# A gated mix of linear attention and a SwiGLU block on one Trainium2 core: the first two x tiles loaded as two half-height DMAs on two queues, and the large weights in more pieces

## The chip, the core and the metric

The kernel runs on one core of one Trainium2 chip. A core has a matrix engine (TensorE, PE in the profile, its weight loads PEld), a vector engine (VectorE, DVE), an activation engine (ScalarE, ACT), a general engine (GpSimd, POOL) and a small engine that here only issues transfers (SyncE, SP). ACT can issue transfers too. All of them are carried out by the core's 16 DMA engines. Every engine works through its own list of instructions in order and waits on semaphores for the others.

The metric is the time of one execution on the device in microseconds (us). Before the change, the median of three runs is 178.27 us (177.99 to 178.33).

## What is computed

x has 2048 tokens of 512 features, in bf16. The result mixes two branches token by token with a sigmoid gate:

```python
x = A_x
g = _sigmoid((x * gate_w).sum(-1, keepdims=True))
a = _A_ref(x, A_wqkv, A_wo)          # linear attention, 32 heads of 16
b = _B_ref(x, B_w1, B_w3, B_w2)      # (silu(x @ w1) * (x @ w3)) @ w2, 1376 hidden
return g * a + (1 - g) * b
```

In branch A, q and k go through phi(t) = (t + 1 where t > 0, else exp(t)) + 1e-6; the attention is linear (k and v are summed over all tokens into one small matrix for each head), divided by a denominator, and multiplied by wo.

## The kernel before

The tokens are cut into 16 tiles of 128 (t = 0 to 15), and into 4 blocks of 4 tiles. The 512 features are 4 chunks of 128 (kc = 0 to 3). The order of instructions on every engine is the order of the text: the schedule is written by hand.

*Loads.* They stand at the top, lines 121 to 158, nearly all on SP's queue (`dq`). The first is x_first (line 129): the first 256 tokens, 2 KB in each of 128 partitions, 256 KB, into the tile xN. Then come four pieces of wqk, the q and k columns of the attention weights, one for each kc (line 126), 14 transposing loads of x for tiles 2 to 15 (xT, line 123) with three plain loads of x (xN, line 141) between them, the gate column and the 96 last columns of w1 and w3 (wr, lines 143 to 147), and then the large weights: w1 and w3 in one DMA of 1280 KB each (line 150, a loop whose `cuts` are (0, KC)), wv, wo (lines 151, 152), w2 in one DMA of 1280 KB (line 154) and w2x (line 156). On ACT's queue there is one load, a small one of 12 KB: touch (line 133), the first 16 columns of the later wqk chunks, which nothing computes with. In ACT's program it stands behind a table load and a tiny activation (act_pre, line 130).

The framework that builds the kernel gives every DMA, from either queue, one of eight semaphores in turn. A DMA is issued only when the DMA that used its semaphore before it, eight places earlier, has landed. There are 72 DMAs in all.

*Start.* TensorE runs 13 warm-up matmuls on a constant (line 359), then transposes the first two tiles of x itself by multiplying xN with the identity (line 365, six of these at first, two later). VectorE and ScalarE copy the results into xT, and the first projections follow (line 183): for each kc, the k and q matmuls of tiles 0 and 1 in the order of lines 386 to 401, each kc needing its piece of wqk.

*First stage* (to about 46 us). For each tile: q and k projections (line 183), phi on ACT and DVE (lines 196 to 201), the running sum of phi(k) on POOL (line 215), and the products of x and phi(k) summed over all tokens (line 231).

*Second stage.* For each block of 512 tokens, ten steps of the SwiGLU block (lines 303 and 309 read w1 and w3), and in the first block the small matrices of the attention (line 447 reads wv, line 462 reads wo). The denominators come from zaccb, POOL's last sum, over SP's transposing DMA of line 421, then zrow (426) and zpk (427), and end in the transposed and scaled queries pqT (line 345). Then four output tiles (line 475 reads pqT, line 492 reads w2, line 278 w2x), mixed on DVE (line 498) and stored from SP (line 508).

Of the kernel before, what the change touches and what calls it, by code (L numbers as in the profile page):

```python
# [16 lines left out]
def kernel(  # L17
# [17 lines left out]
    nc = tc.nc  # L35
    P = nc.NUM_PARTITIONS
# [5 lines left out]
    KC = D // P  # L42
# [4 lines left out]
    FC = F // P  # L47
# [15 lines left out]
    w1_r = B_w1.rearrange("(kc d) f -> d kc f", d=P)  # L63
    w3_r = B_w3.rearrange("(kc d) f -> d kc f", d=P)
# [15 lines left out]
        out=bmask[:], in_=bmask[:], pattern=[[-Dh, HPC], [0, Dh]], compare_op=ALU.is_ge,  # L80
# [3 lines left out]
        out=bmask[:], in_=bmask[:], pattern=[[Dh, HPC], [0, Dh]], compare_op=ALU.is_ge,  # L84
# [22 lines left out]
    xN = consts.tile([P, NT, D], BF16, name="xN")  # L107
# [6 lines left out]
    w1 = consts.tile([P, KC, F0], BF16, name="w1")  # L114
    w3 = consts.tile([P, KC, F0], BF16, name="w3")
    w2 = consts.tile([P, FC, D], BF16, name="w2")
    xT = consts.tile([P, KC, S], BF16, name="xT")
    act_pre = consts.tile([P, 1], BF16, name="act_pre")
    dq = nc.sync
# [6 lines left out]
        dq.dma_start(out=wqk[:, kc, :], in_=wqkv_r[:, kc, 0 : 2 * D])  # L126

    x_first = x2d[0 : 2 * P, :].rearrange("(p j) d -> p j d", j=2)
    dq.dma_start(out=xN[:, 0:2, :], in_=x_first)  # L129
    nc.scalar.activation(out=act_pre[:], in_=warm[:, 0:1], func=ACT.Exp)  # L130

    touch = consts.tile([P, KC - 1, 16], BF16, name="touch")
# [9 lines left out]
    with nc.allow_non_contiguous_dma(reason="gate column"):  # L142
        dq.dma_start(
            out=wr[:, :, 2 * FR : NR], in_=gate_w.rearrange("(kc d o) -> d kc o", d=P, o=1)
        )
    dq.dma_start(out=wr[:, :, 0:FR], in_=w1_r[:, :, F0:F])
    dq.dma_start(out=wr[:, :, FR : 2 * FR], in_=w3_r[:, :, F0:F])
    for w, w_r, cuts in ((w1, w1_r, (0, KC)), (w3, w3_r, (0, KC))):
        for a, b in zip(cuts, cuts[1:]):
            dq.dma_start(out=w[:, a:b, :], in_=w_r[:, a:b, 0:F0])  # L150
    dq.dma_start(out=wv[:], in_=wqkv_r[:, :, 2 * D : 3 * D])
    dq.dma_start(out=wo[:], in_=A_wo.rearrange("(kc d) n -> d kc n", d=P))
    w2_r = B_w2[0:F0, :].rearrange("(fc f) d -> f fc d", f=P)
    dq.dma_start(out=w2[:], in_=w2_r)
    w2x_r = B_w2[F0:F, :].rearrange("(i r) d -> i (r d)", i=RP)
    dq.dma_start(
        out=w2x[:].rearrange("p r d -> p (r d)"),
        in_=w2x_r[None].to_broadcast([TPB, RP, RG * D]),
# [442 lines left out]
```

## Time and profile before

| | |
|---|---|
| median of three runs | 178.27 us (177.99 to 178.33) |
| the profiled execution's own time | 177.74 us |
| its span, first to last instruction | 176.0 us |
| SP's queue: x_first issued / issuing of w2x ends | 0.81 / 36.9 us |
| x_first from issue to landing | 2.8 us |
| wqk, four pieces, from issue to landing | 3.1, 3.7 (median), 4.1 us |
| w1, w3 from issue to landing | 7.5, 10.3 us |
| granted TensorE clock | 1.00 |

The profile is that of one execution. A row of the chain or of the timeline has the start in us from the span's beginning, the length in us, the engine (SPq and ACTq are the issuing of DMAs on SP and ACT), the line of the code, and what is written from what; "x13" means that thirteen such instructions are merged; a bracket at the end tells how long the engine had been idle and what ended that. A row of stretches has the stretch, its length, the busy time of PE, PEld, DVE, ACT and POOL with the number of instructions, the granted clock, the busy share of the DMA engines and the GB/s that they moved.

### The profile page before, as it was taken

Reading aid. Unit: us, or ns where it says so; the run is one execution under the profiler, and the core shown is the slowest. Engines: PE = TensorE matmul, PEld = TensorE weight load, DVE = VectorE, ACT = ScalarE, POOL = GpSimd, SP = SyncE. Lnnn points to the kernel's source line nnn. Section 1 sums busy time; section 2 is a strip of 40 time slices with the busy share of each in tenths; the row PEclk is TensorE's granted clock in tenths of the full one; section 3 lists DMA queues with packets and bytes.
Section 4 is the critical chain, followed back from the end, with each engine's and each line's share of the span. In section 5 each row is a group of like instructions: output and inputs, shape, how many; then the busy total and the mean of one; then the engine's idle time right before and its main releaser. Section 6 shows DMA issues by size and latency. Waiting matters only on the chain.

```text
span 176.0 us, 2668 instructions
## 1 busy us (share of the span) xinstructions
PE 171.3 (97%) x952; PEld 82.4 (47%) x969; DVE 110.5 (63%) x207; ACT 59.1 (34%) x109; POOL 63.3 (36%) x106
## 2 busy tenths in 40 slices
PE   8999999999999999999999999999999999999993
PEld 5444444444456443444444466444444444444453
DVE  0399788888764899777343477853435775344363
ACT  4364544544753533322433101224226122422000
POOL 5087656656300668586300044540000662000000
DMA  5988969997205112323200013330000233000001
GB/s 172 277 197 207 164 123 237 403 352 231 78 4 56 22 30 41 78 63 91 58 0 0 0 34 84 84 89 0 0 4 0 60 89 89 4 0 0 30 30 60
DMA packets 29360, 15.58 MB, mean 88 GB/s; under 512 B 21156, under 2 KB 27556, under 8 KB 29348
## 3 DMA queue, kind: packets, MB, share of 16 engines
q1 hardware_dynamic: 28948, 15.41, 35.1%
q8 instruction: 7, 0.11, 0.3%
q10 hardware_dynamic: 400, 0.01, 0.1%
q14 instruction: 5, 0.04, 0.1%
HBM read 8.86 MB, written 2.10 MB: 62 GB/s over the span
## 4 chain that ended last, share of the span: by engine, by line
PE 95%; DMA 2%; issue 1%; SPq 0%; DVE 0%
PE bank L303 20%; PE bank L492 20%; PE bank L309 19%; PE bank L183 16%; PE bank L231 8%; PE bank L475 8%; PE bank L245 3%; DMA wqk<-in_A_wqkv_dram 2%; PE bank L278 2%; PE bank L447 0%; SPq L129 0%; PE bank L462 0%; DVE o L498 0%; PE bank L365 0%
## 5 line engine op out<-in xcount | busy, mean ns | idle before, releaser
L315 DVE TENSOR_TENSOR hT<-bank,sg 128x512 bf16<-128x512 f32 x40 | 27.3, 682 | 31.0 <-PE bank L309 28.9
L303 PE MATMUL bank<-xT,w 128*128 128x512 bf16 x158 | 40.8, 379 | 0.2
L309 PE MATMUL bank<-xT,w 128*128 128x512 bf16 x156 | 40.5, 379 | 0.2
L314 ACT ACTIVATE sg<-bank 128x512 bf16<-128x512 f32 x40 | 23.9, 597 | 45.9 <-PE bank L303 45.9
L492 PE MATMUL bank<-w,hT 128*128 128x512 bf16 (+2 forms) x176 | 37.0, 355 | 0.5 <-issue 0.3
L337 POOL TENSOR_TENSOR pqs<-pq,rden 128x512 bf16<-128x512 bf16 x16 | 16.9, 1057 | 54.3 <-issue 46.8
L183 PE MATMUL bank<-wqk,xT 128*128 128x512 bf16 x126 | 30.2, 379 | 0.1
L215 POOL TENSOR_TENSOR zacc<-zacc,pk 128x128 f32<-128x128 f32 x56 | 23.3, 447 | 10.4 <-DVE pk L201 10.4
L492 PEld LDWEIGHTS <-hT 128*128 128x128 bf16 x180 | 16.7, 98 | 18.4 <-issue 0.8
L309 PEld LDWEIGHTS <-w 128*128 128x128 bf16 x160 | 15.7, 98 | 18.9
L303 PEld LDWEIGHTS <-w 128*128 128x128 bf16 x160 | 15.5, 98 | 18.2 <-issue 0.2
L498 DVE SCALAR_TENSOR_TENSOR o<-bank,omg_all,aga 128x512 bf16<-128x512 f32 (+2 forms) x18 | 12.4, 692 | 14.5 <-PE bank L492 11.7
L183 PEld LDWEIGHTS <-xT 128*128 128x128 bf16 x128 | 12.5, 98 | 14.9 <-issue 0.3
L322 POOL TENSOR_TENSOR pr<-pq,zb 128x512 f32<-128x512 bf16 x16 | 18.4, 1155 | 0.1
L231 PE MATMUL bank<-pk,xN 128*128 128x512 bf16 x62 | 16.3, 379 | 0.2
L475 PE MATMUL bank<-M,pqT 128*128 128x512 bf16 x61 | 15.6, 379 | 0.1
L196 ACT ACTIVATE eq<-bank 128x512 bf16<-128x512 f32 x16 | 9.4, 597 | 16.0 <-PE bank L183 14.9
L201 DVE SCALAR_TENSOR_TENSOR pk<-bank,emk 128x512 bf16<-128x512 f32 x16 | 11.1, 692 | 1.6
L196 ACT ACTIVATE ek<-bank 128x512 bf16<-128x512 f32 x16 | 9.4, 597 | 6.5 <-PE bank L183 6.5
L201 DVE SCALAR_TENSOR_TENSOR pq<-bank,emq 128x512 bf16<-128x512 f32 x16 | 11.1, 692 | 0.5
L326 DVE TENSOR_REDUCE den<-pr 128x32 f32<-128x512 f32 x16 | 10.8, 676 | 0.0
L231 PEld LDWEIGHTS <-xN 128*128 128x128 bf16 x64 | 6.3, 98 | 7.5
(54 smaller groups left out, 95.6 us busy)
## 6 DMA issues: line engine op xcount, KB each, us to landing
w<-in_B_w_dram SPq DMA_DIRECT2D x3, 1280.0 KB, 10.3
out_dram<-o SPq DMA_DIRECT2D x15, 128.0 KB, 1.9
wqk<-in_A_wqkv_dram SPq DMA_DIRECT2D x4, 256.0 KB, 3.7
xN<-in_A_x_dram SPq DMA_DIRECT2D x1, 1024.0 KB
xN<-in_A_x_dram SPq DMA_DIRECT2D x2, 256.0 KB, 2.9
xN<-in_A_x_dram SPq DMA_DIRECT2D x1, 512.0 KB, 4.2
wv<-in_A_wqkv_dram SPq DMA_DIRECT2D x1, 512.0 KB, 11.2
wo<-in_A_wo_dram SPq DMA_DIRECT2D x1, 512.0 KB, 12.2
```

The lines of the kernel that those rows point to most:

```text
L183: nc.tensor.matmul(ps[:], lhsT=xT[:, kc, t * P : (t + 1) * P], rhs=w[:, kc, :], start=(kc == 0), stop=(kc == KC - 1),)
L196: nc.scalar.activation(out=e[:], in_=ps[:], func=ACT.Exp)
L201: nc.vector.scalar_tensor_tensor(out=dst, in0=ps[:], scalar=0.0, in1=em[:], op0=ALU.max, op1=ALU.add)
L215: nc.gpsimd.tensor_tensor(out=(zaccb if t == NT - 1 else zacc)[:, cs], in0=zacc[:, cs], in1=pk[t][:, cs], op=ALU.add,)
L231: nc.tensor.matmul(bank[kc][:], lhsT=xN[:, t, kc * P : (kc + 1) * P], rhs=pk[t][:], start=(t == 0), stop=(t == NT - 1),)
L303: nc.tensor.matmul(g_ps[:], lhsT=w1[:, kc, fs], rhs=xT[:, kc, tok], start=(kc == 0), stop=(kc == KC - 1),)
L309: nc.tensor.matmul(u_ps[:], lhsT=w3[:, kc, fs], rhs=xT[:, kc, tok], start=(kc == 0), stop=(kc == KC - 1),)
L314: nc.scalar.activation(out=sg[:], in_=g_ps[:], func=ACT.Silu)
L315: nc.vector.tensor_tensor(out=hT[tb][:, fc, :], in0=u_ps[:], in1=sg[:], op=ALU.mult)
L322: nc.gpsimd.tensor_tensor(out=pr[t][:], in0=pq[:, t, :], in1=zb[:], op=ALU.mult)
L475: nc.tensor.matmul(ps[:], lhsT=pqT[:, c, ts], rhs=M2[:, c, :], start=(c == 0), stop=(c == KC - 1),)
L492: nc.tensor.matmul(ps[:, 0 : cs.stop - cs.start], lhsT=hT[tb][:, fc, tt * P : (tt + 1) * P], rhs=w2[:, fc, cs], start=(fc == 0 and not sta ...
```

## The change

The load of x_first becomes two DMAs: partitions 0 to 63 on SP's queue, and partitions 64 to 127 on ACT's, where it stands ahead of the table load and of touch. w1 and w3 come in four DMAs each, one for each kc, instead of one. w2 comes in two, of five chunks each, instead of one. The bytes and their places stay the same; the number of DMAs goes from 72 to 80. TensorE's first weight load from xN waits for two semaphores instead of one, and its first matmuls on w1, w3 and w2 wait for the pieces that they read. Nothing else in the order of any engine changes.

```diff
     x_first = x2d[0 : 2 * P, :].rearrange("(p j) d -> p j d", j=2)
-    dq.dma_start(out=xN[:, 0:2, :], in_=x_first)
+    dq.dma_start(out=xN[0 : P // 2, 0:2, :], in_=x_first[0 : P // 2])
+    nc.scalar.dma_start(out=xN[P // 2 : P, 0:2, :], in_=x_first[P // 2 : P])
     nc.scalar.activation(out=act_pre[:], in_=warm[:, 0:1], func=ACT.Exp)
...
-    for w, w_r, cuts in ((w1, w1_r, (0, KC)), (w3, w3_r, (0, KC))):
+    for w, w_r, cuts in ((w1, w1_r, range(KC + 1)), (w3, w3_r, range(KC + 1))):
         for a, b in zip(cuts, cuts[1:]):
             dq.dma_start(out=w[:, a:b, :], in_=w_r[:, a:b, 0:F0])
...
     w2_r = B_w2[0:F0, :].rearrange("(fc f) d -> f fc d", f=P)
-    dq.dma_start(out=w2[:], in_=w2_r)
+    for a, b in ((0, FC // 2), (FC // 2, FC)):
+        dq.dma_start(out=w2[:, a:b, :], in_=w2_r[:, a:b, :])
```

## The prediction

> **What bounds the kernel now.** I read the page first: busy times, then the chain that ended last.
>
> ```profile
> PE 171.3 (97%) x952; PEld 82.4 (47%) x969; DVE 110.5 (63%) x207; ACT 59.1 (34%) x109; POOL 63.3 (36%) x106
> ...
> PE 95%; DMA 2%; issue 1%; SPq 0%; DVE 0%
> ```
>
> TensorE is busy for 171.3 of 176.0 us, and the only transfer in the chain is 2%. So next I read that chain in order of time over the first 16 us, which shows where the 2% lies (start, length, what):
>
> ```profile
> 0.81 0.39 SPq L129
> 1.20 0.06 issue
> 1.26 3.11 DMA wqk<-in_A_wqkv_dram
> 4.37 0.04 issue
> 4.41 1.02 PE bank L183 x4
> 5.43 0.11 PE bank L365 x2
> 5.54 3.60 PE bank L183 x16
> ```
>
> After 4.41 us everything is TensorE work, one matmul behind the other. Eight matmuls take 1.73 us all along the chain, 0.216 each. The sixteen here should take 3.45 and take 3.60, so 0.15 us is lost in them. The timeline of the first 14 us says where, and what TensorE did before:
>
> ```profile
> 0.84 2.93 PE L359 MATMUL bank<-const-bfloat16-1.0 128*128 128x256 bf16 x13 [0.84 <-PEq L585]
> 0.86 0.43 ACTq L133 DMA_DIRECT2D touch<-in_A_wqkv_dram  x1
> ...
> 3.64 0.55 PEld L365 LDWEIGHTS <-xN 128*128 128x128 bf16 x6 [0.35 <-DMA xN<-in_A_x_dram]
> 3.65 0.72 PE L365 MATMUL bank<-ident,xN 128*128 128x128 bf16 x6
> ...
> 6.83 1.82 PEld L183 LDWEIGHTS <-xT 128*128 128x128 bf16 x9 [0.27 <-issue]
> ```
>
> Thirteen warm-up matmuls run until the x tiles land; the first weight load out of xN then starts at 3.64 after 0.35 us of waiting. The 0.15 us lie at 6.83: the fourth piece of wqk is issued at 2.67 and lands up to 4.1 us later (the longest of line 126), at 6.78. From 6.83 on the matmuls follow each other to the end. The change therefore can act on the end in two ways: by moving the start of that stream, or by making a weight so late that it opens a hole in it.
>
> **The change, part by part.** *The first x DMA in two halves.* One issue of 0.39 us on SP (line 129) becomes one of 64 rows on SP and one of 64 rows on ACT. Per issue I take 0.39 to 0.43 (lines 129 and 133); SP has as many issues in this stretch as before, so wqk starts at 1.26 as before. On ACT, by the order of its instructions, the new issue stands ahead of the table load and act_pre (0.80 to 2.30 now); these end 0.43 later, at 2.73, and touch starts about 0.45 later. ACT's first work for the path comes at 4.08, so 1.3 us of cover remain. Without that cover the cost would be the 0.43.
>
> What counts is when the later half lands, since TensorE's first load of xN now waits for both. At best both land before the warm-up ends. The thirteen take 2.93 us, one takes 0.42, so they start 0.209 apart, the last at 3.35, and the next could start at 3.56 instead of 3.65: a gain of at most 0.09. At worst the half on ACT's queue is as late as touch, today's only DMA there: issued at 0.86 and landed after 3.0 us although it is only 12 KB, while x with 256 KB needs 2.8. Issue at 0.82, 3.0 us, and 128 KB at the best rate seen here (413 GB/s, next fence), 0.32, give 4.14, which is 0.50 after the 3.64 of now. I take 0.0: the same 256 KB pass the same engines, and touch came late because x's bytes lay before it, not because the queue slept; in the stretch 2.5 to 3.1 us, in which x's last bytes pass, ACT's queue already moves 156 packets.
>
> ```profile
> 1.80:2.00 0.20, 0.20 (x3) 0.14 (x2) 0.00 (x0) 0.20 (x1) 0.14 (x1) 1.00 0.14 31
> 2.00:2.20 0.20, 0.20 (x3) 0.14 (x2) 0.00 (x0) 0.19 (x2) 0.19 (x1) 1.00 0.45 133
> 2.20:2.40 0.20, 0.20 (x3) 0.14 (x2) 0.00 (x0) 0.10 (x1) 0.15 (x1) 1.00 0.93 143
> 2.40:2.60 0.20, 0.20 (x3) 0.14 (x2) 0.00 (x0) 0.00 (x0) 0.17 (x1) 1.00 0.77 246
> 2.60:2.80 0.20, 0.20 (x3) 0.14 (x2) 0.00 (x0) 0.00 (x0) 0.12 (x2) 1.00 0.81 317
> 2.80:3.00 0.20, 0.20 (x3) 0.14 (x2) 0.00 (x0) 0.00 (x0) 0.20 (x1) 1.00 1.12 413
> ```
>
> These are stretches of 0.2 us; the last column is GB/s, the one before it the DMA engines' share. The load starts slowly and reaches its full rate only at 2.8, and 256 KB have passed by about 3.0.
>
> The Trainium skill (SBUF — State Buffer, section "Can I just issue two DMAs to hit both halves?") speaks against this part: a tile in partitions 0 to 63 reaches half of the memory's ports, and two concurrent DMAs on the two halves measured only 6% over one. No transfer of 64 partitions is in this trace, so nothing here shows it; by that rule the sum would be the first rival's, below.
>
> *wqk behind it.* The fourth piece sets the 0.15 us at 6.83. If it lands earlier the most to gain is that 0.15; if x's engines are held longer, it slips by as much. I take 0.0: the bytes ahead of it are the same.
>
> *w1 and w3 in four pieces, w2 in two.* Seven more issues on SP at 0.506 (line 150) are 3.5 us of queue. w1 lands at 26.4 + 7.5 = 33.9, w3 at 26.9 + 10.3 = 37.2, wv at 38.7, w2 at 30.3 + 13.5 = 43.8; they are first used at 45.9 (line 303), 46.8 (309), 52.7 (447) and 67.0 (492). So 3.5 us more leave at least 6 us for each. Each issue waits until the DMA eight places before it has landed (the order of SP's instructions with their waits). Before, all those were long landed; now wv, wo, both halves of w2 and w2x wait for pieces of w1 and w3. If the last of them, w2x, had to wait for all of w3 (37.2, plus its own 2.95 of issuing, line 156), SP would be free at 40.2, with 3.5 more at 43.7. What stands behind it is the transpose of zaccb:
>
> ```profile
> SPq L421 <- POOL zaccb L215: 9.1, 1, 9.1
> ```
>
> SP sits 9.1 us waiting for POOL there, until 46.1. So this costs nothing; were the cover gone, zaT, zpk and pqT would slide, and the first pqT (63.6 + 2.4 = 66.0) still has 4.9 us until line 475 reads it at 70.9. The first matmuls on w1 and w3 get a wait on each piece; waits already satisfied do not show in the stream today (the 0.216 hold at every wait on an xT). With 80 DMAs for 72, eight more, every DMA behind w2x keeps the semaphore it had.
>
> Sum: 0.0 for x (from -0.09 to +0.50), 0.0 for wqk (from -0.15 to +0.15), 0.0 for the weights: 176.0 + 0.0 in the span and 1.7 around it, 177.74 in the profiled execution's own time. That execution was 0.5 below the median of the three runs, 178.27, so in their terms 178.3.
>
> **The rivals.** *Halves at half rate: slower.* Place: the load of x. If a DMA on 64 partitions can use half of the path, the six rows above are capped at half of 413, 207 GB/s. By 2.4 us 61 KB have passed below that cap; the other 201 KB then need 0.97 us and end at 3.37 instead of 3.02: +0.35. If the slow start is not cover but comes on top (1.1 us now against 0.63 at 413, so 0.47 lost; 1.27 at 207), they end at 3.66: +0.64. wqk lies behind on the same engines and slips as far, so all of it reaches the end: 178.6 to 178.9, say 178.75. It decides from the moment x lands after 3.64, one for one, and can be measured from 0.36 later, 4.0. For it: the rows from 2.6 on do run above 207. Against: the first half of the load does not, and the two halves together use everything. The rule named above is this case.
>
> *ACT's queue starts late: slower.* The half on ACT lands at 4.14 as worked out. wqk does not slip then, so its 0.15 is absorbed: +0.35, 178.6. For it: touch's 3.0 us. Against: touch stands behind act_pre in ACT's order, the new DMA stands first.
>
> *A better start: faster.* The two queues fill the slow rows 1.8 to 2.6 together, x lands before the warm-up ends and wqk before 6.6: -0.24 in all, 178.0. More than this is only possible if the start of an ordinary run is worse than that of the profiled one, which the 0.5 between them leaves open. Against: the warm-up's 3.56 is a floor.
>
> *The pieces hold SP beyond 46.1 by more than the 4.9 us of slack.* Each microsecond beyond is one of the end; 179 or more. Against: six microseconds of margin ahead of that.
>
> **How the numbers follow.** No change worth measuring 0.44; half rate 0.28; ACT late 0.11; better start 0.15; SP held 0.02. A measurement of this kernel can tell about 0.2%, 0.36 us, from nothing. Of the likeliest, 0.38 lies within that and 0.03 on each side; of half rate 0.20 above it, of ACT late 0.07; of the better start 0.12 below; SP held above. Faster 0.15, within 0.53, slower 0.32. The likeliest alone would be 178.0 to 178.5 (-0.24 to +0.2). The range goes to 178.85 to hold the most of the two slower cases, and to 177.85 for the better start with the spread of the three runs (0.34) under it.
>
> **What would show it.** In the profile after: the first weight load out of xN at 3.6 (right), about 4.0 to 4.3 (half rate, with wqk's pieces later too), about 4.1 with wqk where it was (ACT late), or 3.55 (better start); the idle time before the fourth piece of wqk; SP's wait for zaccb still above 2 us; no idle time at the first matmuls of lines 303, 309, 447 and 492. A hole in the stream after 7 us, or a total that moves without the first 7 us moving, would make the prediction wrong.

## The result, and the profile after

| | before | after |
|---|---|---|
| median of six executions | 178.19 us (177.83 to 178.33) | 180.98 us (179.08 to 181.24) |
| the profiled execution | 177.74 us | 181.11 us |
| its span | 176.0 us | 179.3 us |

The changed kernel takes 1.0123 times as long as the one before (95% interval 1.0099 to 1.0147). It is slower, and it lies well above the range of the prediction. Its executions fall into two groups, two at 179.1 us and four from 180.93 to 181.24; the profile is one of the upper group. The ratios in this document are those on record, which are not quotients of the medians (180.98/178.19 would be 1.0157).

The page after has the same make-up as before, but the transfer in the chain that ended last has grown from 2% to 3%:

```profile
PE 173.8 (97%) x969; PEld 82.9 (46%) x969; DVE 110.3 (62%) x207; ACT 59.1 (33%) x109; POOL 63.2 (35%) x106
...
PE 95%; DMA 3%; SPq 0%; DVE 0%; issue 0%
```

VectorE, ScalarE and GpSimd are busy as long as before, within 0.2 us. TensorE is busy 2.5 us longer with the same work. Some matmul records are missing before (hence x952), which makes part of that; but 1.5 us of it are on the line of the projections (30.2 before, 31.7 now) for two records more, so TensorE was slower there. The chain of waits over the first 16 us says where (start, length, what):

```profile
1.44 4.92 DMA wqk<-in_A_wqkv_dram
...
6.40 1.87 PE bank L185 x4
...
8.48 3.87 PE bank L185 x16
...
13.00 0.86 PE bank L185 x4
```

Two things are new. The first projection (line 185, line 183 before) starts at 6.40 instead of 4.41, because wqk's first piece takes 4.92 us instead of 3.11 and is issued 0.18 later. And the first four projections then take 1.87 us, where four of the same kind take 0.86 at 13.00. The timeline of the first 14 us shows what came ahead of it (start, length, engine, line, what is written from what; the bracket is the idle time before and what ended it):

```profile
0.81 0.58 SPq L129 DMA_DIRECT2D xN<-in_A_x_dram  x1
0.81 0.55 ACTq L130 DMA_DIRECT2D xN<-in_A_x_dram  x1
...
1.44 2.23 SPq L126 DMA_DIRECT2D wqk<-in_A_wqkv_dram  x4
...
4.18 0.56 PEld L367 LDWEIGHTS <-xN 128*128 128x128 bf16 x6 [0.88 <-DMA xN<-in_A_x_dram]
...
6.40 1.87 PE L185 MATMUL bank<-wqk,xT 128*128 128x512 bf16 x4 [1.39 <-DMA wqk<-in_A_wqkv_dram]
```

Each half of x takes 0.55 to 0.58 us to issue, where the whole took 0.39. The first weight load out of xN starts at 4.18 instead of 3.64, and TensorE then waits another 1.39 us for wqk.

Nothing behind this adds to it. I take the first projection of tile 3, the twenty-first matmul of its line, as a mark: it starts at 9.63 us before and at 12.84 after, and from there to the end of the span are 166.41 us before and 166.42 after. In all seventeen profiles of this study that rest lies between 166.4 and 166.7 us. So all but 0.3 us of the difference between any two of these profiles is made before the mark or outside the span, and the experiments can be read there. Of the 3.37 us between the two profiled executions, 1.99 is the later first projection, 1.21 is the slower stretch from it to the mark (6.43 instead of 5.22 us), 0.01 is the rest, and 0.15 lies outside the span (1.85 instead of 1.70 us).

### The profile page after: what moved, and what is told of

Its sections match the earlier page's. It is cut to its first block, busy times and chain, and to the rows that moved or that the text cites. A ratio compares the mean times of both kernels' runs of the same rounds, so it can differ in the third digit from the quotient of the medians.

```text
span 179.3 us, 2693 instructions
## 1 busy us (share of the span) xinstructions
PE 173.8 (97%) x969; PEld 82.9 (46%) x969; DVE 110.3 (62%) x207; ACT 59.1 (33%) x109; POOL 63.2 (35%) x106
## 4 chain that ended last, share of the span: by engine, by line
PE 95%; DMA 3%; SPq 0%; DVE 0%; issue 0%
PE bank L494 19%; PE bank L305 19%; PE bank L311 19%; PE bank L185 16%; PE bank L477 8%; PE bank L233 8%; PE bank L247 3%; DMA wqk<-in_A_wqkv_dram 3%; PE bank L280 2%; PE bank L449 0%; SPq L129 0%; PE bank L464 0%; DVE o L500 0%; PE bank L367 0%
## 5 line engine op out<-in xcount | busy, mean ns | idle before, releaser
L305 PE MATMUL bank<-xT,w 128*128 128x512 bf16 x160 | 41.1, 379 | 0.0
L311 PE MATMUL bank<-xT,w 128*128 128x512 bf16 x160 | 41.1, 379 | 0.0
L494 PE MATMUL bank<-w,hT 128*128 128x512 bf16 (+2 forms) x180 | 37.5, 355 | 0.0
L185 PE MATMUL bank<-wqk,xT 128*128 128x512 bf16 x128 | 31.7, 391 | 1.4 <-DMA wqk<-in_A_wqkv_dram 1.4
L477 PE MATMUL bank<-M,pqT 128*128 128x512 bf16 x64 | 16.1, 379 | 0.0
```

Source lines behind the costliest of these rows:

```text
L185: nc.tensor.matmul(ps[:], lhsT=xT[:, kc, t * P : (t + 1) * P], rhs=w[:, kc, :], start=(kc == 0), stop=(kc == KC - 1),)
L305: nc.tensor.matmul(g_ps[:], lhsT=w1[:, kc, fs], rhs=xT[:, kc, tok], start=(kc == 0), stop=(kc == KC - 1),)
L311: nc.tensor.matmul(u_ps[:], lhsT=w3[:, kc, fs], rhs=xT[:, kc, tok], start=(kc == 0), stop=(kc == KC - 1),)
L477: nc.tensor.matmul(ps[:], lhsT=pqT[:, c, ts], rhs=M2[:, c, :], start=(c == 0), stop=(c == KC - 1),)
L494: nc.tensor.matmul(ps[:, 0 : cs.stop - cs.start], lhsT=hT[tb][:, fc, tt * P : (tt + 1) * P], rhs=w2[:, fc, cs], start=(fc == 0 and not sta ...
```

## The experiments

The theory at the start was that the two halves of x make it land later and wqk with it; the rivals were the pieces of w1, w3 and w2, ACT's queue, and TensorE's own rate. In each group below the kernels ran on one chip beside the kernel before (medians 178.25, 178.20, 178.13 and 178.27 us). The diffs are against the kernel before, unless said.

### Which part: e1 to e4

e1 has only x's part of the change, e2 only that of the weights:

```diff
 # e1_x_only
-    dq.dma_start(out=xN[:, 0:2, :], in_=x_first)
+    dq.dma_start(out=xN[0 : P // 2, 0:2, :], in_=x_first[0 : P // 2])
+    nc.scalar.dma_start(out=xN[P // 2 : P, 0:2, :], in_=x_first[P // 2 : P])
```

> Only the load of x is split in two halves on two queues; w1, w3 and w2 stay whole. Theory A (the whole loss comes from the split of x, in the first 9 us): 179 to 181.2, the first weight load from xN at about 4.2 and the first projection at 5 to 6.4. Rival B (the pieces of w1, w3 and w2 and their waits take a part): 178.2 to 178.6.

```diff
 # e2_w_only, against the kernel after
-    dq.dma_start(out=xN[0 : P // 2, 0:2, :], in_=x_first[0 : P // 2])
-    nc.scalar.dma_start(out=xN[P // 2 : P, 0:2, :], in_=x_first[P // 2 : P])
+    dq.dma_start(out=xN[:, 0:2, :], in_=x_first)
```

> Only w1, w3 and w2 are cut in pieces; x is one DMA of 128 partitions as before. Theory A: 178.2 within 0.3, with no idle time at the first matmuls on w1, w3 and w2. Rival B: 179 or more.

e3 puts both halves on SP's queue, e4 keeps the two queues but cuts x by columns, so that each DMA has all 128 partitions with rows of 1 KB:

```diff
 # e3_both_sp
-    dq.dma_start(out=xN[:, 0:2, :], in_=x_first)
+    dq.dma_start(out=xN[0 : P // 2, 0:2, :], in_=x_first[0 : P // 2])
+    dq.dma_start(out=xN[P // 2 : P, 0:2, :], in_=x_first[P // 2 : P])
 # e4_cols
-    dq.dma_start(out=xN[:, 0:2, :], in_=x_first)
+    dq.dma_start(out=xN[:, 0, :], in_=x_first[:, 0, :])
+    nc.scalar.dma_start(out=xN[:, 1, :], in_=x_first[:, 1, :])
```

> x in the same two halves of 64 partitions, but both on SP's queue, one after the other; weights whole. Theory C (a transfer of 64 partitions runs at half rate): x lands 0.3 to 0.7 later than the 3.60 of before, 178.6 to 179.5. Theory D (the loss comes from issuing on two queues at once, which delays the half on SP and the wqk pieces behind it): x and wqk land within 0.4 of before (one more issue of SP, 0.4, stands ahead of wqk), 178.2 to 178.7, and no late landing of the first wqk piece.

> x in two DMAs on the two queues, but each of all 128 partitions with one token row of 1 KB in each; weights whole. Theory C (64 partitions are slow): x lands as before at about 3.6, 178.2 within 0.4. Theory D (two queues at once are slow): x lands at 4.1 or later and the first wqk piece after 5, 179 or more.

| | median, us | ratio to before | first load of xN | first projection |
|---|---|---|---|---|
| e1 | 179.36 | 1.0065 [1.0032, 1.0097] | 4.02 | 5.25 |
| e2 | 178.40 | 1.0006 [0.9984, 1.0028] | 3.62 | 4.38 |
| e3 | 180.47 | 1.0107 [1.0076, 1.0138] | 4.54 | 5.18 |
| e4 | 178.60 | 1.0007 [0.9988, 1.0026] | 3.71 | 4.63 |

The cost is in x's part alone: neither the weights' pieces nor two DMAs on two queues (e4) cost anything that can be told from nothing. Two halves on one queue cost no less than on two (the intervals of e3 and e1 overlap), so ACT's queue is not what makes the change slow. Both theories for e3 had expected less, at most 179.5. The profiled execution of e3 is the fastest of its six (179.04 us, the others took 180.12 to 180.63). Its chain of waits shows five issues in a row, two of x and three of wqk:

```profile
0.81 0.58 SPq L129
...
1.45 0.57 SPq L130
...
2.07 0.58 SPq L126
...
2.70 0.42 SPq L126
...
3.17 0.43 SPq L126
...
3.64 4.34 DMA wqk<-in_A_wqkv_dram
...
8.02 2.32 PE bank L184 x10
```

Both halves are dear to issue (0.58, 0.57), and so is the first piece of wqk behind them (0.58, the next ones 0.42 and 0.43), which is a DMA of 128 rows as it was. The fourth piece is issued at 3.64 instead of 2.67 and holds TensorE until 8.02.

### touch, and the rate of TensorE: e5 to e8

e5 is e1 and e6 the kernel before, both without touch, which nothing computes with:

```diff
 # e5_x_notouch (with the edit of e1) and e6_before_notouch
-    touch = consts.tile([P, KC - 1, 16], BF16, name="touch")
-    nc.scalar.dma_start(out=touch[:], in_=wqkv_r[:, 1:KC, 0:16])
```

> x split as in the change, weights whole, and the load touch (which nothing computes with) left out. If touch, which ACT now issues at 1.45 beside SP's first wqk piece, is what makes that piece's issue 0.81 long and holds some of the DMA engines, the issue falls to about 0.4 to 0.6, wqk lands by 5, and the time falls from the 179.4 of the split alone to 178.6 to 179. If touch has no part in it: 179.2 to 179.6.

> The kernel before without touch, as the control of the run above: 178.2 within 0.3 if touch does nothing for wqk; 178.6 or more if the wqk pieces get later without it.

e5 took 178.92 us, 1.0053 [1.0019, 1.0087], and e6 178.40, 1.0011 [0.9998, 1.0024]. In e5 the first piece of wqk still takes 0.81 us to issue, as in e1. So touch is not what makes the issues dear; without it the ratio is not told apart from e1's. The time fell where it had been expected if touch mattered (178.6 to 179), but the sign that was to go with it, a shorter issue, did not come.

e7 fills the two holes of the changed kernel with warm-up matmuls, and e8 makes a hole in the kernel before and leaves its DMAs alone:

```diff
 # e7_after_fill, against the kernel after
-    warm_step(13)
+    warm_step(16)
...
+    warm_step(6)
     for kc in range(2):
 # e8_few_warm
-    warm_step(13)
+    warm_step(6)
```

> The changed kernel with TensorE kept busy on the constant while it waits: 16 warm-up matmuls instead of 13, and 6 more between the transposes and the first projection. Nothing is computed differently. Theory E (the holes at the start also keep TensorE at half rate for longer): the matmuls of line 185 are at 0.216 apart by 7 us at the latest, and the time falls from 181.0 by 0.8 to 1.5, to 179.5 to 180.2. Rival (the rate has nothing to do with the holes): 180.8 to 181.5, since fillers only add work.

> The kernel before with 6 warm-up matmuls instead of 13, so that TensorE has a hole from 2.1 to 3.6 us and all the DMAs are untouched. Theory E: x and wqk land as before, but the first projections run 0.43 apart until 7 to 9 us, and the time is 179 to 180.3. Rival: 178.2 within 0.3.

e8 took 179.52 us, 1.0076 [1.0049, 1.0103]. The chain of e8:

```profile
0.81 2.87 DMA xN<-in_A_x_dram
...
4.55 1.79 PE bank L183 x4
...
6.55 5.03 PE bank L183 x16
```

x lands at 3.68 instead of 3.60 and the first projection starts at 4.47 instead of 4.41 (timeline), yet the sixteen behind the first four take 5.03 us instead of 3.60: with seven warm-up matmuls fewer, and so a hole in TensorE's work from 2.3 to 3.7 us, its matmuls start 0.427 us apart, not 0.216, until about 9.7 us. The reverse is e7, whose chain is:

```profile
5.06 0.91 PE bank L361 x6
5.97 0.86 PE bank L185 x4
...
6.95 3.45 PE bank L185 x16
```

Without holes the first four take 0.86 and the sixteen 3.45, the full rate from the start, although the first projection starts late (5.81 in the timeline). e7 took 179.20 us (178.83 to 179.63), 1.0058 [1.0038, 1.0077]. That is less than either expectation for it (179.5 or more). It has no execution in the upper group, where the changed kernel had four of six; on another chip, though, it had two of ten (e12, below), and at that share six executions without one come about one time in four. Also, its fillers last longer than the wait that they fill, and its median is no better than that of e12 (179.10). So e7 shows the rate in one execution, not a mended kernel.

The granted clock does not show the slow stretch. These are stretches of the changed kernel (the columns are those of the stretches before the prediction; the clock is third from the end):

```profile
6.40:8.20 1.80, 1.80 (x6) 0.70 (x6) 0.00 (x0) 0.00 (x0) 0.00 (x0) 1.00 1.55 149
9.30:12.30 3.00, 3.00 (x16) 1.37 (x14) 1.19 (x3) 1.08 (x2) 0.14 (x1) 1.00 0.83 207
```

Six matmuls in 1.8 us, two of them small, and sixteen in 3.0 us, both at 1.00. The Trainium skill (TensorE: Matmul & The Clock Gate, section "Part 1: The HAM clock gate (the "warmup" mystery)") says that the array runs at half its clock until enough work has been seen in a window that runs freely, and that the number of slow matmuls therefore differs from execution to execution. The factor of two agrees with the starts here (0.427 us apart against 0.216), and so does the spread; that it is this gate no run here shows.

### How x is cut: e9 to e12

```diff
 # e9_wqk_act: x whole on SP; wqk's pieces 0 and 2 on ACT's queue, 1 and 3 on SP's
-    def load_wqk(kc):
-        dq.dma_start(out=wqk[:, kc, :], in_=wqkv_r[:, kc, 0 : 2 * D])
+    def load_wqk(kc, q=dq):
+        q.dma_start(out=wqk[:, kc, :], in_=wqkv_r[:, kc, 0 : 2 * D])
...
     dq.dma_start(out=xN[:, 0:2, :], in_=x_first)
+    load_wqk(0, nc.scalar)
...
-    for kc in range(KC):
-        load_wqk(kc)
+    load_wqk(1)
+    load_wqk(2, nc.scalar)
+    load_wqk(3)
 # e10_cols_w, against the kernel after: all of the change, but x by columns
-    dq.dma_start(out=xN[0 : P // 2, 0:2, :], in_=x_first[0 : P // 2])
-    nc.scalar.dma_start(out=xN[P // 2 : P, 0:2, :], in_=x_first[P // 2 : P])
+    dq.dma_start(out=xN[:, 0, :], in_=x_first[:, 0, :])
+    nc.scalar.dma_start(out=xN[:, 1, :], in_=x_first[:, 1, :])
 # e11_96_32
-    dq.dma_start(out=xN[:, 0:2, :], in_=x_first)
+    dq.dma_start(out=xN[0:96, 0:2, :], in_=x_first[0:96])
+    nc.scalar.dma_start(out=xN[96:P, 0:2, :], in_=x_first[96:P])
```

> Two queues used without cutting anything: x is one DMA on SP as before, the first and third piece of wqk go on ACT's queue, the second and fourth on SP's. If two queues in themselves cost nothing, x lands at 3.6 to 3.9, the fourth piece by 6.5, and the time is 177.9 to 178.4; it could gain the 0.15 of the wait for the fourth piece. If the queue that gets its first bytes later holds up the other (as the half on SP did behind the half on ACT), x lands at 4 or later and the time is 178.8 or more.

> The whole change with its 80 DMAs on the two queues, but x cut by token rows: two DMAs of all 128 partitions with 1 KB in each. Theory C (half-height transfers are the cause: dearer to issue and later to start): issues of 0.4 for both x DMAs and the first wqk piece, x landed by 3.9, time 178.2 to 178.8. Theory D (two queues, or 80 DMAs): 179.5 or more.

> x cut in 96 partitions on SP and 32 on ACT, weights whole: measures what the height does to an issue. Theory C as a matter of any height below 128: both issues 0.55 or longer and the first wqk piece's too, 179 to 180. If only the number of rows counts, 96 rows cost less than 0.4 and 32 less than 0.3, and the time is 178.2 to 178.8.

e12 is the changed kernel once more:

> The changed kernel once more, for a second profile of its start. Theory A with E: x again lands near 4.1 and the first wqk piece's issue again takes 0.8; whether some DMA engines are late with the first piece again, and when the matmuls reach 0.216 apart, says what separates its times near 179.1 from those near 181.0: each 0.1 of a later first projection and each 0.2 of half rate beyond it cost 0.1.

| | median, us | ratio to before | first load of xN | first projection |
|---|---|---|---|---|
| e9 | 179.31 | 1.0071 [1.0044, 1.0097] | 4.17 | 4.84 |
| e10 | 178.23 | 1.0005 [0.9984, 1.0026] | 3.68 | 4.64 |
| e11 | 178.78 | 1.0042 [1.0029, 1.0055] | 3.83 | 4.51 |
| e12 | 179.10 | 1.0060 [1.0033, 1.0087] | 4.01 | 5.38 |

e10 has 80 DMAs, both queues and all the pieces, and is not told apart from the kernel before. Its timeline has no dear issue:

```profile
0.80 0.40 ACTq L130 DMA_DIRECT2D xN<-in_A_x_dram  x1
0.81 0.39 SPq L129 DMA_DIRECT2D xN<-in_A_x_dram  x1
...
1.25 1.84 SPq L126 DMA_DIRECT2D wqk<-in_A_wqkv_dram  x4
...
3.68 0.63 PEld L367 LDWEIGHTS <-xN 128*128 128x128 bf16 x6 [0.39 <-DMA xN<-in_A_x_dram]
```

So what costs is the cut of x by rows. e11, cut at 96, issues in 0.40 and 0.42 us, as a load of 128 rows does, which neither expectation for it had (0.55 or more, or less than 0.4 and 0.3); it delays wqk's issues not at all. None of its executions took more than 178.98 us, but it is still 0.4% slower, which is not told apart from the 0.6% of the halves on the same chip (e12), with the first load of x at 3.83 (3.68 with the cut by columns). Why a cut by rows lands later when its issue is not dear is open. e9 shows another way to lose: x is whole and issued at 0.80, but wqk's first piece comes beside it from ACT's queue, and x lands at 4.12 instead of 3.60.

e12 repeats the changed kernel on another chip: slower again, but by half as much. Eight of its ten executions took 178.55 to 179.34 us and two 180.39 and 180.56, so it has the same two groups in other shares. Its interval does not even meet that of the first result, 1.0060 [1.0033, 1.0087] against 1.0123 [1.0099, 1.0147], for the same kernel: an interval here tells of one set of executions on one chip, and a difference of this size between kernels on different chips is no evidence. Its profile is of the lower group:

```profile
1.44 3.90 DMA wqk<-in_A_wqkv_dram
...
5.38 1.02 PE bank L185 x4
...
6.52 3.45 PE bank L185 x16
```

The issues are the same as in the first profile of the changed kernel (wqk begins at 1.44). What differs is that wqk's first piece takes 3.90 us instead of 4.92, and that TensorE is at its full rate almost from the start (1.02 and 3.45 instead of 1.87 and 3.87). The trace has sixteen completions for each such load, as many as there are DMA engines, and I take each for the end of one engine's part. In that first profile twelve of those of the piece had come by 4.97 us and four came at 6.08 to 6.36; in e12 all had come by 5.34.

Late completions are not the only way into the upper group. The profile of e1 is of an execution of 180.38 us whose first piece of wqk landed at 5.21, and it lost its time to the slow matmuls:

```profile
1.44 3.77 DMA wqk<-in_A_wqkv_dram
...
5.25 1.87 PE bank L184 x4
...
7.33 4.17 PE bank L184 x16
```

From its first projection to the mark it took 6.73 us, where e12 took 5.08.

### Is it 64 rows: f1 to f3

```diff
 # f1_wqk_half: only wqk's fourth piece is cut, both halves on SP
-        dq.dma_start(out=wqk[:, kc, :], in_=wqkv_r[:, kc, 0 : 2 * D])
+        for rows in (slice(0, P // 2), slice(P // 2, P)) if kc == KC - 1 else (slice(0, P),):
+            dq.dma_start(out=wqk[rows, kc, :], in_=wqkv_r[rows, kc, 0 : 2 * D])
 # f2_80_48
-    dq.dma_start(out=xN[:, 0:2, :], in_=x_first)
+    dq.dma_start(out=xN[0:80, 0:2, :], in_=x_first[0:80])
+    nc.scalar.dma_start(out=xN[80:P, 0:2, :], in_=x_first[80:P])
 # f3_64_1k: four DMAs of 64 rows with 1 KB each, two on each queue
-    dq.dma_start(out=xN[:, 0:2, :], in_=x_first)
+    for rows, q in ((slice(0, P // 2), dq), (slice(P // 2, P), nc.scalar)):
+        for j in range(2):
+            q.dma_start(out=xN[rows, j, :], in_=x_first[rows, j, :])
```

> x is one DMA as before; the fourth piece of wqk comes as two DMAs of 64 rows on SP. If 64 rows as such are dear to issue: 0.55 to 0.6 each, the fourth piece lands 0.5 to 0.9 later, 178.5 to 179. If only x's halves are dear (their rows lie in one piece in memory, those of wqk do not): 0.40 to 0.44 each, 178.2 to 178.6.

> x cut in 80 rows on SP and 48 on ACT, weights whole. If 64 rows alone are dear: issues of 0.39 to 0.43, first wqk piece issued by 1.3 and landed by 4.7, 178.4 to 178.9. If a cut near the middle is dear: 0.5 or more and 179 or more.

> x in four DMAs of 64 rows with 1 KB in each row, two on SP and two on ACT, weights whole. If 64 rows as such are dear: about 0.55 for each of the four and wqk starts to issue at 2 or later, 179.5 or more. If it is that 64 rows of 2 KB lie in one piece in memory: about 0.4 each, wqk issued from 1.65 on, 178.5 to 179.2.

f1 took 178.81 us, 1.0031 [1.0012, 1.0050]; f2 178.56, 1.0026 [1.0007, 1.0046]; f3 180.47, 1.0156 [1.0090, 1.0223], from four executions. The issues in the timelines of f2 and then of f3:

```profile
0.80 0.42 ACTq L130 DMA_DIRECT2D xN<-in_A_x_dram  x1
0.80 0.40 SPq L129 DMA_DIRECT2D xN<-in_A_x_dram  x1
```

```profile
0.80 1.20 ACTq L131 DMA_DIRECT2D xN<-in_A_x_dram  x2
0.80 1.47 SPq L131 DMA_DIRECT2D xN<-in_A_x_dram  x2
```

80 and 48 rows are issued like 128; 64 rows of 1 KB are as dear as 64 rows of 2 KB (0.56 to 0.61 each on ACT, 0.59 and 0.82 on SP). In f1 the two halves of a piece of wqk take 0.56 and 0.59 where the whole one takes 0.43. So 64 rows are dear to issue in x and in wqk, with 1 or 2 KB in a row, on either queue, and DMAs of 32, 48, 80, 96 and 128 rows in the same places are not. Why is not settled, and the number of rows is not all: the plain loads of x behind the transposing ones have 128 partitions, and in the kernel before each takes 0.58 too:

```profile
5.80 0.58 SPq L141 DMA_DIRECT2D xN<-in_A_x_dram  x1
```

f2 also tells the two delays apart. Its first load of x starts at 3.98, nearly as late as that of e1 (4.02), but wqk is issued at 1.26 instead of 1.44, and its first projection starts at 4.61 instead of 5.25. So in these profiles it is wqk, more than x, that moves the first projection. What e11 and f2 still lose shows in their chains, which wait for wqk's second piece: its last completion came at 5.95 and 5.81, with the other fifteen in by 5.16 and 5.18; before, all sixteen were in by 5.17. The control e6, which is not told apart from the kernel before, has such late completions too, so whether the cut brings them is open.

## Why the prediction was wrong

The forecast was no change, 178.3 us. The step that failed is "Per issue I take 0.39 to 0.43 (lines 129 and 133); SP has as many issues in this stretch as before, so wqk starts at 1.26 as before." No DMA of 64 rows was in the trace, and I priced it by issues of 128 rows. It takes 0.58 on SP and 0.55 on ACT, and the issue behind it on SP 0.81 instead of 0.41: wqk starts at 1.44, its four issues take 2.23 instead of 1.84, and its fourth goes out at 3.24 instead of 2.67. The bounds of the sum had no such term. The top of the range lay 0.55 above the forecast; the medians of e12 and of the kernel beside it differ by 0.97 (179.10 and 178.13), and in the first profile late DMA engines and slow matmuls, which had no term either, came on top. The issue is not all of it: e11, whose issues are as before, is 0.4% slower, and that part has no shown cause.

Point by point:

- *x, 0.0 (from -0.09 to +0.50).* It was +0.54 in the first profile, where the first weight load out of xN moved from 3.64 to 4.18, just above the upper end, and +0.37 in e12 (4.01). It did not reach the end by itself, since TensorE then waited longer for wqk. But that end was argued from ACT's queue being late, and it was SP's half that was late. The DMA view of the changed kernel shows it, from 2.0 to 2.7 us and then from 2.7 to 3.4 (q1 is SP's queue, q10 ACT's; packets, MB, share of the 16 engines):

```profile
q10 hardware_dynamic: 51, 0.10, 35.9%
q1 hardware_dynamic: 3, 0.01, 2.2%
```

```profile
q1 hardware_dynamic: 95, 0.16, 86.0%
q10 hardware_dynamic: 420, 0.04, 45.5%
```

ACT's half passes first (51 packets, three from SP), then SP's; most of the 420 packets on ACT's queue by then are touch's small ones. ACT's half lands 2.8 us after its issue and SP's 3.3. So the two queues did not share the first stretch as "A better start" had it, either.
- *wqk, 0.0 (±0.15).* It was +0.97 in e12 (first projection from 4.41 to 5.38) and +1.99 in the first profile. Of the 0.97, 0.58 is the issue of its first piece, which ends at 2.25 (1.44 and 0.81) instead of 1.67 (1.26 and 0.41); the other 0.39 came in the transfer. The other 1.02 of the 1.99 go with the four late DMA engines, and why they were late is open. The working looked at the fourth piece alone; it was the first that TensorE waited for.
- *The rate of TensorE: a term that was missing.* I took 0.216 for every matmul from 4.41 on, because the profile shows it there. That profile was a lucky one: e2 starts its projections 0.03 us earlier than the kernel before and has the first four at 1.80 instead of 1.02, and the mark 0.93 us later. This is of the kind and size of the 0.5 us between the profiled execution and the median, which I had noted and not explained; that this is its cause was not tried. In the first profile of the changed kernel the stretch up to the mark was 1.21 us longer, in e12 0.14 shorter (5.08 us), with holes in both. e8, all of whose executions took 179.0 us or more, shows that a hole can bring the slow matmuls about; it does not do so each time.
- *w1, w3 and w2 in pieces, 0.0.* Right, by e2 (1.0006) and e10 (1.0005). The 3.5 us more of SP's queue did not come: the last issue, that of w2x, ends at 36.1 instead of 36.9, because the later issues took less (wo 0.84 instead of 2.20, w2 2.98 instead of 3.66, w2x 1.73 instead of 2.95). SP's wait for zaccb is still there, and longer, since zaccb came 3.2 later and SP was free 0.9 earlier:

```profile
SPq L423 <- POOL zaccb L217: 13.1, 1, 13.1
```

That satisfied waits cost nothing, and that eight more DMAs disturb no semaphore behind them, follows from the same two runs and from the 166.42 us behind the mark.
- *The table load 0.43 later on ACT.* It was later by 0.59 (act_pre ended at 2.89 for 2.30), and still hidden: ACT's first copy of xT waits for TensorE.

Of the rivals that act at the start, *halves at half rate* gave the time nearest to the result (178.75), and its sign in the profile came true, the first load at 4.0 to 4.3 with wqk later too. Its mechanism did not. It capped the rows at 207 GB/s, but in the first profile the row in which the 64 rows on ACT end and those on SP begin has 451:

```profile
2.40:2.60 0.20, 0.20 (x3) 0.14 (x2) 0.00 (x0) 0.20 (x1) 0.18 (x1) 1.00 0.51 205
2.60:2.80 0.20, 0.20 (x3) 0.14 (x2) 0.00 (x0) 0.19 (x2) 0.12 (x2) 1.00 1.22 451
```

That row has both halves in it, each of which might have had its 207. In e12 one half is alone: from 2.4 to 2.6 us only ACT's queue moves packets, 30 of them, and its 64 rows pass at 307 GB/s:

```profile
2.40:2.60 0.20, 0.20 (x3) 0.14 (x2) 0.00 (x0) 0.20 (x1) 0.18 (x1) 1.00 0.77 307
```

So the halves passed above the cap. They started late: the packets of ACT's half after 2.0 us and those of SP's after 2.6, where those of the whole load had started after 1.8. A sign that two mechanisms share does not tell them apart; the rate did. *ACT's queue starts late* was wrong as well, since ACT's half landed first (3.56 against 4.07). But what I put against it did not hold: touch did not wait for act_pre, it was issued at 0.86, while the table load ran (0.80 to 2.08). The Trainium skill's advice (SBUF — State Buffer, "Can I just issue two DMAs to hit both halves?"; DMA: Bandwidth & Descriptors, "Rules for kernel authors") not to cut a load into partition halves held (1.0123 and 1.0060). The second page adds that several queues save only issue time; here the halves cost more of it (0.55 to 0.58 us each, for 0.39).

No version of this study beat the kernel before. The best, e10 and e2, equal it.

## What to carry to other kernels

Price a DMA by a row of its own shape: a cut of x that leaves every DMA all its 128 partitions cost nothing measurable here, one at 80 or 96 partitions 0.3 to 0.4%, and one at 64 0.5 to 1.2%. At the head of a kernel, whose first load and first weights feed an engine that is then busy to the end, each tenth of a microsecond counts, and a hole in TensorE's work can cost more than its own length: in e8 the first projection started 0.06 us later, and the median rose by 1.3 us. Look at the spread of the executions and at more than one chip before you trust a start that a single profile shows.

## What was not expected of the hardware

- At the head of the kernel the issue of a DMA of 64 rows took 0.55 to 0.61 us, and the issue behind it on the same queue 0.53 to 0.82, against 0.39 to 0.43 for 32, 48, 80, 96 and 128 rows. Further on, loads of 128 rows took 0.51 (w1, w3) and 0.58 (line 141) as well. Open: why.
- TensorE's matmuls of 512 columns start 0.427 us apart instead of 0.216 for a time that differs from execution to execution, until 9.7 us in e8 and not at all in the profile of the kernel before, while the granted clock reads 1.00.
- A second queue can delay the load that is needed first: in e9, with wqk's first piece on ACT's queue, ACT's moved 0.22 MB and SP's 0.21 from 2.4 to 3.6 us, and x landed at 4.12 instead of 3.60.
- The time around the span went with the number of DMAs on ACT's queue: 1.70 to 1.74 us in all profiles with none or one, 1.84 to 1.88 with two, 2.04 with three (e9 and f3). No run tried it by itself; for the changed kernel it is 0.15 of the 3.37 us.
- Four of the sixteen completions of a 256 KB load came 1.1 to 1.4 us after the others, in one profile, for wqk's first piece and much the same for its second and third. What decides it stays open, and so do the shares of the two groups on a chip.
